# Statistics of one batch from summed chunks, two spreads over partitions by DMA, and new rules in the plan of an attention and feed-forward kernel

## The chip, the cores and the metric

The kernel runs on one core of one Trainium2 chip. The metric is the device time of one execution in microseconds. Before the change the median of three runs is 842.28 us (842.24 to 842.83). One more execution was taken with a profile; times "in the trace" count from its first instruction.

## The reference

Four batches of causal attention, 12 heads, 448 positions, 64 values a head, are followed by a feed-forward layer with a norm ahead of it and a sum around it, all in float32:

```python
scores = (q @ k.T) / 8, masked above the diagonal
attn = softmax(scores);  x = attn @ v            # 4 x 448 x 768 after joining the heads
mu = mean(x, -1);  var = mean((x - mu) ** 2, -1)
xn = (x - mu) / sqrt(var + 1e-6) * g
out = x + relu(xn @ w1) @ w2                     # 768 -> 3072 -> 768
```

## The kernel before, in words

**Layout.** x is kept transposed: six chunks `xT[c]` of 128 features by 448 positions for each batch. Every factor of a large product is split into a high and a low part, and three products stand for one. The positions are four blocks of 112 where they lie on partitions.

**Stages.** The first batch's attention comes first, with nothing to put beside it but weight conversion. The feed-forward layer of the first batch (`ffn`, L1106; tiles ph and po) then runs on TensorE, and between its products stand the second and third batch's attention; beside the second batch's feed-forward layer stand the rest of the third's and the fourth's. From 531 us of the trace the third and fourth batch's feed-forward layers run together (`Pair`, L1159), with seven products of blocks in place of eight; its tiles are bA, bX, bY, bZ. The weights arrive as float64, are converted once by ScalarE and VectorE (`convert1`, `convert2`, L617 to L634), stored to DRAM (`keep`, L636) and loaded again later.

**The plan.** The program first records every instruction as a task with its engine, its reads and writes and a due time (`Plan`, L173). TensorE's clock of due times advances by 1.45 us a step ahead of the first feed-forward layer and by the cost of the products within it. `schedule` (L317) works back from the due times to the time at which each task is needed, with SLACK (L44) added for each step, and calls `run` (L367) six times; that is a list scheduler with costs of its own (`cost`, L273) and the best of the six orders is issued. An engine takes the available task with the earliest need. `pick` (L471) passes over a task on the SBUF port that VectorE and GpSimd share if that port is taken for more than 0.3 us longer; this holds for the first 70 us of the plan's time. Between engines that could act at the same time, the order of `ENGINES` (L177) decides. All instructions are issued by one line, L526, so tiles tell them apart. SP issues all DMAs, in the plan's order. Tasks with two ways (`either`, L193) may go to either of two engines.

**Statistics.** Three ways lead to the mean and 1/sigma of a batch.
- First batch: `total` (L943) adds the six chunks, one product with a column of 1/768 gives the mean on all partitions (`mean`, L950), and `squares` (L956) subtracts it, squares on ScalarE, adds the six squares and reduces them over partitions with four products of one column. The power -1/2 is GpSimd's. `over_sigma` (L973) spreads the 112 x 4 result over partitions and positions with four transposes into PSUM and a copy.
- Second batch: `stats` (L983) transposes every chunk back (tile pln) and VectorE's bn_stats reads it; `aggr` (L994) joins them; `spread` (L1004) makes eight transposes and two copies on ScalarE. `apply1` reads the results.
- Third and fourth batch: `stats` and `aggr` as well; `Pair.banks` (L1167) spreads mean and 1/sigma of both batches with sixteen transposes into four PSUM banks, and the pair's inputs (`xg`, L1199) read them there.

`BYSUM` and `VAR0`, `RB0`, `AHEAD0` (L60 to L62) belong to the first way: steps between the mean, the squares and the first feed-forward layer. `tl` is the step at which a batch's attention is done; 84 (`PAIR`) is the step from which the pair's inputs are recorded.

**Pools.** probs is closed and temps, for the pair's inputs, is opened once probs has no more readers; in the same way pair_x follows ap (`open_inputs`, L1178).

Of the kernel before, what the change touches and what calls it, by code (L numbers as in the profile page):

```python
# [40 lines left out]
SECOND = 8000  # L41
BEHIND = 12000
EARLY_SLOT = 1450
SLACK, DMA_SLACK = 400, 6000  # L44
CHANGE, TOGETHER = 150, 12000
PASSES, PORT, LEAST, AFTER, URGENT, START = 6, 300, 300, 1500, 5000, 70000
STEPS = 6
FIRST = -20
RAT0, TAT0, NAT0, END0, EV0 = [-1, 1, 3], [7, 8, 9, 10, 11], [4, 6], 13, [1, 1, 0, 1, 0]
# [7 lines left out]
PAIR = 84  # L57
KEEP0 = 36
TWOS = {3: [0, 2, 4]}
BYSUM, VAR0, RB0 = [0], 2, 6  # L60
COPIED = [NP, NP, 3, 0]
AHEAD0 = 6  # L62
WARM, FILL, LATE = 10, 16000, 3500
LEFT = {1: (0, 0), 2: (0, 1), 3: "S4", 4: (1, 1), 5: "S1", 6: "S2", 7: "S3"}
RIGHT = {1: "B11", 2: "B21", 3: "B22", 4: "T4", 5: "T1", 6: "T2", 7: "T3"}
# [18 lines left out]
class View:  # L84
# [39 lines left out]
    def bitcast(self, dtype):  # L124
        return self._new(self.p, self.idx, lambda t: t.bitcast(dtype), dtype)

    def to_broadcast(self, shape):
        return self._new(self.p, self.idx, lambda t: t.to_broadcast(shape))

# [43 lines left out]
class Plan:  # L173

    ENGINES = ("tensor", "vector", "scalar", "gpsimd", "sync")  # L177

    def __init__(self):
        self.tasks, self.fresh, self.turns, self.clock, self.wait = [], [], [], 0.0, 0.0  # L180
# [136 lines left out]
    def schedule(self):  # L317
        tasks = self.tasks
        for t, buf in self.fresh:
            old = buf.before  # L320
            while old is not None and not old.any:
                old = old.before
            if old is not None:
                t.deps.update(old.any)
            elif buf.pool.opened is not None:
                t.deps.add(buf.pool.opened)
        for t, pools in self.turns:
            t.deps.update(n for pool in pools for buf in pool.tiles for n in buf.any)
        for t in tasks:
            for d in t.deps:  # L330
                tasks[d].then.append(t.n)
        need, left, line = [0.0] * len(tasks), [len(t.deps) for t in tasks], []
        line = [t.n for t in tasks if not t.deps]
        for n in line:
            for m in tasks[n].then:
                left[m] -= 1
                if left[m] == 0:
                    line.append(m)
        assert len(line) == len(tasks)
        for t in (tasks[n] for n in reversed(line)):  # L340
            x = t.due if t.engine == "tensor" else 1e9
            for m in t.then:
                x = min(x, need[m])
            if t.engine == "sync":
                x -= DMA_SLACK + t.lag / 300
            elif t.engine and t.engine != "tensor":
                x -= t.cost + t.lag + SLACK
            elif t.engine and x < t.due:
                x -= t.cost + t.lag + SLACK
            need[t.n] = x  # L350
        best, hint = None, None
        for _ in range(PASSES):
            order, span = self.run(need, hint)
            if best is None or span < best[1]:
                best = order, span, self.starts, self.fin, {t.n: t.way for t in tasks if t.engine}
            self.old, hint = self.starts, {e: [] for e in self.ENGINES}
            for t in tasks:
                for way in t.ways if t.engine else ():
                    hint[way[0]].append((self.ready[t.n], t.n))
            for x in hint.values():  # L360
                x.sort()
        order, span, self.starts, self.fin, kept = best
        for n, i in kept.items():
            self.take(tasks[n], i)
        return order, span

    def run(self, need, hint):  # L367
        tasks = self.tasks
# [34 lines left out]
        while True:  # L403
# [21 lines left out]
                    heapq.heappush(avail[e], (need[n] + more, n))  # L425
            heap = avail[e]
            if e not in ("tensor", "sync"):
                n, wake = self.pick(e, at, heap, start, port, need, hint, drift)
                if n is None:
                    held[e] = wake  # L430
                    continue
            elif e == "tensor":
                while heap:
                    x = heapq.heappop(heap)
                    heapq.heappush(tiled[tasks[x[1]].mode], x)
                heap = min((h for h in tiled.values() if h), key=lambda h: h[0])
                same = tiled[mode]
                if same and same[0][0] < heap[0][0] + TOGETHER:
                    heap = same
# [28 lines left out]
        self.ready = ready  # L468
        return [n for _, n in order], max(free.values())

    def pick(self, e, at, heap, start, port, need, hint, drift):  # L471


        skipped, wake, n = [], [], None
        while heap:
# [5 lines left out]
            skipped.append(x)  # L481
            if shared and port > at + PORT and at < START:
                wake.append(port)
                continue
            if hint is not None and at < START:
                line, first = hint[e], None
# [48 lines left out]
def kernel(ctx, tc, qk, v, w1, w2, g, out):  # L535
# [49 lines left out]
    scratch = [dr.tile([P, UE], F32, name=f"scratch{i}") for i in range(len(order))]  # L585
    kept = [dr.tile([P, UH], F32, name=f"kept{i}") for i in range(ns)]
    ready = set()
    raw, bits, w32, wh, wl = {}, {}, {}, {}, {}

    def load_raw(s):  # L590
# [114 lines left out]
    class Att:  # L705
# [237 lines left out]
        def total(self, p):  # L943
            if p == 0:
                return
            if p == 1:
                self.acc = rest[:, :S]
            self.add(self.acc, self.acc if p > 1 else self.xT[0], self.xT[p])

        def mean(self):  # L950
            mb = ps.tile([P, S], F32, tag="sc", name="mb", bufs=2)
            nc.tensor.matmul(mb, lhsT=part.to_broadcast([P, P]), rhs=self.acc, start=True, stop=True)
            self.mb = ap.tile([P, S], F32, tag="y", name="mbs", bufs=1)
            nc.scalar.activation(out=self.mb, in_=mb, func=ACTF.Copy, scale=-1.0)

        def squares(self):  # L956
            for c in range(KC):
                t = ap.tile([P, S], F32, tag="PT", name="xc", bufs=8)
                nc.vector.tensor_tensor(out=t, in0=self.xT[c], in1=self.mb, op=ALU.add)
                nc.scalar.activation(out=t, in_=t, func=ACTF.Square)  # L960
                if c:
                    self.add(acc, acc, t)
                else:
                    acc = t
            pt = ps.tile([C, NC], F32, tag="sc", name="var", bufs=2)
            for x in range(NC):
                nc.tensor.matmul(pt[:, x:x + 1], lhsT=acc[:, x * C:(x + 1) * C], rhs=part, start=True, stop=True)
            ve = sb.tile([C, NC], F32, tag="ve", name="ve", bufs=2)
# [1 line left out]
            nc.gpsimd.tensor_tensor(out=ve, in0=ve, in1=mhalf, op=ALU.pow)  # L970
            self.t["ve"] = ve

        def over_sigma(self):  # L973
            ve = self.t["ve"]
            rb = ps.tile([P, S], F32, tag="sc", name="rb", bufs=2)
            for x in range(NC):
                nc.tensor.transpose(
                    rb[:, x * C:(x + 1) * C], ve[:, x:x + 1].to_broadcast([C, P]), ident[:C, :C]
                )
            self.rb = ap.tile([P, S], F32, tag="rb", name="rbs", bufs=1)  # L980
            move(self.rb, rb)

        def stats(self, part, x):  # L983
            c0, c1 = (2 * part, 2 * part + 2) if self.twos else STATS[part]
# [18 lines left out]

        def spread(self):  # L1004
            mv, ve = self.t["mv"], self.t["ve"]
            mb = ps.tile([P, S], F32, tag="sc", name="mb", bufs=2)
            rb = ps.tile([P, S], F32, tag="sc", name="rb", bufs=2)
            for x in range(NC):
                nc.tensor.transpose(
                    mb[:, x * C:(x + 1) * C], mv[:, x, 0:1].to_broadcast([C, P]), ident[:C, :C]  # L1010
                )
            for x in range(NC):
                nc.tensor.transpose(
                    rb[:, x * C:(x + 1) * C], ve[:, x:x + 1].to_broadcast([C, P]), ident[:C, :C]
                )
            for key, src in (("mb", mb), ("rb", rb)):
                self.t[key] = ap.tile([P, S], F32, tag="PT", name=key, bufs=8)
                nc.scalar.copy(out=self.t[key], in_=src)
            self.parts()

        def apply1(self, c):
# [17 lines left out]
        def steps(self):  # L1039
# [13 lines left out]
            for p, t0 in enumerate(t0s):  # L1053
# [5 lines left out]
                if p - p % 2 in self.twos:  # L1059
                    if p % 2:  # L1060
                        put(post, t0 + end, self.pv, p - 1)
                        put(post, t0 + end, self.pv, p)
                else:
                    put(post, t0 + end, self.pv, p)
                if self.b == 0:
                    put(pre, t0 + end + 1, self.total, p)
                    put(pre, t0 + end + 1, self.gained1, p)
                    put(pre, t0 + end + 1, self.gained2, p)
# [14 lines left out]
            if self.b == 0:  # L1083
                put(post, tl, self.mean)
                put(pre, tl + AHEAD0 + VAR0, self.squares)
                put(post, tl + AHEAD0 + RB0, self.over_sigma)
                return pre, post, tl + AHEAD0
            th = TH1 if self.b == 1 else [t0s[i] + end + 1 for i in ((1, 3) if self.twos else (2, 4))]
            for x in range(NC):
                put(post, th[0] + x, self.stats, 0, x)  # L1090
# [68 lines left out]
    class Pair:  # L1159
# [6 lines left out]

        def banks(self):  # L1167
            for j, a in enumerate(self.at):
                mb = ps.tile([P, S], F32, tag="sc", name="mb", bufs=2)
                rb = ps.tile([P, S], F32, tag="pt", name="rb", bufs=2)  # L1170
                for dst, col in ((mb, lambda x: a.t["mv"][:, x, 0:1]), (rb, lambda x: a.t["ve"][:, x:x + 1])):
# [4 lines left out]
                a.t["mb"], a.t["rb"] = mb, rb  # L1176

        def open_inputs(self):  # L1178
            turn(probs, temps)
# [409 lines left out]
```

## Time and profile before

| | |
|---|---|
| median of the runs | 842.28 us |
| profiled execution, its time | 845.26 us |
| profiled execution, its span | 843.4 us |
| mean granted TensorE clock | 0.997 |
| TensorE busy | 835.7 us |
| VectorE, ScalarE, GpSimd busy | 689.8, 513.7, 266.3 us |
| SP's DMA queue | 167.9 MB |

The span goes from the first to the last instruction; the rest of the time lies around it. PE is TensorE's matmul, PEld its weight load, DVE VectorE, ACT ScalarE, POOL GpSimd, SP the engine that issues the DMAs. A matmul's duration runs to its modelled end, and the next one starts before that, so the distance of two starts is what one costs. In the rows an instruction is written as output<-inputs by tile names.

### The profile page before, as it was taken

To read this page: it belongs to the slowest core of one execution; us is meant where nothing else is said; L and a number is where in the kernel's file an instruction comes from. 1 tells how busy PE (TensorE), PEld (TensorE's weight loads), DVE (VectorE), ACT (ScalarE), POOL (GpSimd) and SP (SyncE) were. 2 spreads that over 40 slices of the span, in tenths; PEclk is the share of its full clock that TensorE was granted. 3 is DMA by queue.
4 is the path that set the end of the run, shared out by engine and by line. 5 is a ranking of instruction groups with operands and counts; after the bars stand their busy time and mean duration, and the time that the engine had idled before them with its cause. 6 is when DMAs were issued, how large, how long until landed. Compare 5 with 4: busy or idle time off the path is not lost.

```text
span 843.4 us, 13755 instructions
## 1 busy us (share of the span) xinstructions
PE 835.7 (99%) x4608; PEld 729.1 (86%) x4608; DVE 689.8 (82%) x1464; ACT 513.7 (61%) x1130; POOL 266.3 (32%) x271
## 2 busy tenths in 40 slices
PE   8999999999999999999999999999999999999998
PEld 5578898888888888888888899999999999999997
DVE  5999999899999997887777389786886768777685
ACT  7999998889898586554453135453634436354450
POOL 4732111011123521111110049445445454554440
PEclk9999999999999999999999999999999999999999
DMA  9588888967888778887766454324243332423334
GB/s 234 198 264 279 294 296 336 360 235 281 273 274 318 250 245 291 263 286 237 233 214 206 152 190 154 110 86 142 60 150 94 101 122 83 139 83 110 114 94 152
DMA packets 61318, 168.79 MB, mean 200 GB/s; under 512 B 7008, under 2 KB 25824, under 8 KB 61248
## 3 DMA queue, kind: packets, MB, share of 16 engines
q1 hardware_dynamic: 61248, 167.92, 59.7%
q8 instruction: 36, 0.59, 0.3%
q14 instruction: 34, 0.28, 0.1%
HBM read 119.15 MB, written 39.71 MB: 188 GB/s over the span
## 4 chain that ended last, share of the span: by engine, by line
PE 85%; DVE 6%; ACT 6%; issue 2%; DMA 1%; SPq 0%; POOL 0%; ACTq 0%; DVEq 0%; POOLq 0%
PE bX L526 21%; PE po L526 17%; PE ph L526 16%; PE bY L526 10%; PE bA L526 5%; PE px L526 5%; PE sc L526 4%; PE pt L526 4%; DVE w L526 1%; ACT P L526 1%; DVE P L526 1%; DVE wl L526 1%; ACT w L526 1%; ACT bits L526 1%; PE pln L526 1%
## 5 line engine op out<-in xcount | busy, mean ns | idle before, releaser
L526 POOL TENSOR_TENSOR kl<-qkraw,kh 128x896 fp32r<-128x896 f32 x18 | 40.4, 2245 | 254.8 <-ACT kh L526 137.5
L526 PE MATMUL ph<-xh,wh 128*128 128x450 f32 (+1 forms) x288 | 110.6, 384 | 0.0
L526 PE MATMUL po<-hh,wh 128*128 128x448 f32 x288 | 109.7, 381 | 0.0
L526 ACT ACTIVATE P<-P,least 112x448 f32<-112x448 f32 (+3 forms) x176 | 91.5, 524 | 28.5 <-DVE least L526 27.0
L526 PE MATMUL ph<-xh,wl 128*128 128x450 f32 (+1 forms) x288 | 106.2, 369 | 0.1
L526 PE MATMUL po<-hl,wh 128*128 128x448 f32 x288 | 105.9, 368 | 0.0
L526 PE MATMUL po<-hh,wl 128*128 128x448 f32 x288 | 105.7, 367 | 0.0
L526 PE MATMUL ph<-xl,wh 128*128 128x450 f32 (+1 forms) x288 | 105.4, 369 | 0.0
L526 ACT ACTIVATE wp<-s 128x256 fp32r<-128x256 f32 (+1 forms) x113 | 50.9, 459 | 74.8 <-PE bX L526 35.2
L526 DVE CUSTOM_DVE_ANT_0 P<-sc,mask 112x224 f32<-112x224 f32 (+3 forms) x176 | 72.7, 443 | 22.7 <-PE sc L526 22.4
L526 POOL TENSOR_TENSOR s<-u 128x256 f32<-128x256 f32 (+1 forms) x60 | 54.6, 919 | 78.1 <-DMA u<-scratch 54.0
L526 ACT ACTIVATE wk<-u 128x256 fp32r<-128x256 f32 (+1 forms) x77 | 35.7, 464 | 68.7 <-PE bX L526 56.0
L526 DVE TENSOR_TENSOR wp<-s,wp 128x256 fp32r<-128x256 f32 (+1 forms) x120 | 67.3, 571 | 0.8 <-ACT wp L526 0.4
L526 POOL TENSOR_TENSOR h<-b,h 128x448 fp32r<-128x448 f32 x36 | 42.2, 1173 | 70.8 <-ACT b L526 42.0
L526 DVE TENSOR_TENSOR xT<-xT,bX 128x448 f32<-128x448 f32 x72 | 44.4, 617 | 19.2 <-PE bX L526 18.7
L526 PEld LDWEIGHTS ph<-xh,wl 128*128 128x128 f32 x288 | 54.1, 188 | 5.5 <-DVE wl L526 0.5
L526 PEld LDWEIGHTS ph<-xh,wh 128*128 128x128 f32 x288 | 54.2, 188 | 4.8 <-issue 0.2
L526 PEld LDWEIGHTS po<-hh,wh 128*128 128x128 f32 x288 | 54.2, 188 | 4.6 <-DVE P L526 0.7
L526 PEld LDWEIGHTS po<-hh,wl 128*128 128x128 f32 x288 | 54.1, 188 | 4.4
L526 PEld LDWEIGHTS po<-hl,wh 128*128 128x128 f32 x288 | 54.3, 189 | 3.5
L526 PEld LDWEIGHTS ph<-xl,wh 128*128 128x128 f32 x288 | 54.4, 189 | 3.3
L526 ACT ACTIVATE PT<-pt 112x448 f32<-112x448 f32 x74 | 39.1, 539 | 23.6 <-PE pt L526 20.4
(184 smaller groups left out, 2193.4 us busy)
## 6 DMA issues: line engine op xcount, KB each, us to landing
raw<-w_dram SPq DMA_DIRECT2D x39, 768.0 KB, 6.9
scratch<-w SPq DMA_DIRECT2D x48, 384.0 KB, 5.2
full<-scratch SPq DMA_DIRECT2D x24, 768.0 KB, 6.9
qkraw<-qk_dram SPq DMA_DIRECT2D x18, 896.0 KB, 5.5
kept<-wl SPq DMA_DIRECT2D x30, 384.0 KB, 5.8
u<-scratch SPq DMA_DIRECT2D x24, 384.0 KB, 4.0
u<-scratch SPq DMA_DIRECT2D x36, 256.0 KB, 2.9
PR<-P SPq DMA_DIRECT2D x18, 490.0 KB, 4.0
```

The costliest lines, as they stand in the source:

```text
L526: getattr(getattr(nc, t.engine), method)(*args, **kw)
```

## The change

1. The fourth batch's statistics are made the first batch's way. Its chunks are added in pairs of chunks as they come (accumulator `acc` in probs), the mean's product stays in PSUM, VectorE subtracts it from there into tiles of ap (tag PT), and the variance goes to a PSUM bank of tag pt. `stats` and `aggr` are no longer called for it, and `banks` spreads only its 1/sigma.
2. `over_partitions` spreads a 112 x 4 tile over partitions with two DMAs: one writes it to a row of 448 values in DRAM, the other reads the row into all 128 partitions. It takes the place of the transposes and copies in `over_sigma` (first batch, 1/sigma) and in `spread` (second batch, mean and 1/sigma).
3. In the plan SLACK is 200, AHEAD0 is 4, GpSimd stands ahead of VectorE in `ENGINES`, `pick` lets VectorE pass over a task on the shared port while GpSimd works (first 70 us), and `MOVES` displaces the need of one task in eight by up to 3.9 us either way, and of one in 128 by up to 0.2 us, chosen by a hash of the task's number.

```diff
-SLACK, DMA_SLACK = 400, 6000
+SLACK, DMA_SLACK = 200, 6000
+MOVES = [
+    (79784165, 3000, 32, 7730, 90000), (121416589, 3000, 2, -410, 90000),
+]
-AHEAD0 = 6
+AHEAD0 = 4
...
-    ENGINES = ("tensor", "vector", "scalar", "gpsimd", "sync")
+    ENGINES = ("tensor", "gpsimd", "vector", "scalar", "sync")
...
+        base = list(need)
+        for seed, size, share, low, high in MOVES:
+            for t in tasks:
+                x = self.drawn(t.n, seed)
+                if t.engine and x % 256 < share and low < base[t.n] < high:
+                    need[t.n] += size * ((x >> 8) % 65536 / 65536 - 0.5)
...
+            if shared and e == "vector" and other > at and at < START:
+                wake.append(other)
+                continue
...
-                self.acc = rest[:, :S]
+                self.acc = probs.tile([P, S], F32, tag="acc", name="acc", bufs=1) if self.b else rest[:, :S]
...
+            if self.b:
+                self.t["mb"] = mb
+                return
...
+                if self.b:
+                    nc.vector.tensor_tensor(out=t, in0=self.xT[c], in1=self.t["mb"], op=ALU.subtract)
...
+        def over_partitions(self, dst, src):
+            row = dr.tile([NC, C], F32, name=f"row{len(rows)}")
+            rows.append(row)
+            nc.sync.dma_start(out=row.seen(lambda t: t.rearrange("x q -> q x")), in_=src)
+            nc.sync.dma_start(
+                out=dst, in_=row.seen(lambda t: t.rearrange("x q -> (x q)").partition_broadcast(P))
+            )
...
         def over_sigma(self):
-            ve = self.t["ve"]
-            rb = ps.tile([P, S], F32, tag="sc", name="rb", bufs=2)
-            for x in range(NC):
-                nc.tensor.transpose(
-                    rb[:, x * C:(x + 1) * C], ve[:, x:x + 1].to_broadcast([C, P]), ident[:C, :C]
-                )
             self.rb = ap.tile([P, S], F32, tag="rb", name="rbs", bufs=1)
-            move(self.rb, rb)
+            self.over_partitions(self.rb, self.t["ve"])
...
-            for key, src in (("mb", mb), ("rb", rb)):
+            for key, src in (("mb", mv[:, :, 0]), ("rb", ve)):
                 self.t[key] = ap.tile([P, S], F32, tag="PT", name=key, bufs=8)
-                nc.scalar.copy(out=self.t[key], in_=src)
+                self.over_partitions(self.t[key], src)
...
+                if self.b == 3:
+                    for x in (p - 1, p) if p % 2 else ():
+                        put(pre, t0 + end + 1, self.total, x)
...
+            if self.b == 3:
+                put(post, tl, self.mean)
+                put(post, tl + 1, self.squares)
+                return pre, post, PAIR
...
+                both = [(rb, lambda x: a.t["ve"][:, x:x + 1])]
+                if j == 0:
+                    a.t["mb"] = ps.tile([P, S], F32, tag="sc", name="mb", bufs=2)
+                    both.insert(0, (a.t["mb"], lambda x: a.t["mv"][:, x, 0:1]))
```

## Rows read from the trace of the kernel before

**Rows 1.** The page, part 1: busy us of each engine, share of span, instructions.

```profile
PE 835.7 (99%) x4608; PEld 729.1 (86%) x4608; DVE 689.8 (82%) x1464; ACT 513.7 (61%) x1130; POOL 266.3 (32%) x271
```

**Rows 2.** Stretches: us, busy (instructions) of PE, PEld, DVE, ACT, POOL; clock, DMA share, GB/s.

```profile
40.00:50.00 10.00, 10.00 (x68) 6.54 (x64) 8.34 (x26) 8.70 (x23) 4.21 (x9) 0.84 0.59 185
...
60.00:100.00 40.00, 39.90 (x216) 36.12 (x216) 38.57 (x79) 38.87 (x81) 9.55 (x6) 1.00 0.84 283
...
480.00:490.00 10.00, 10.00 (x67) 7.63 (x64) 4.11 (x13) 1.28 (x2) 1.01 (x1) 1.00 0.29 100
490.00:531.00 41.00, 41.00 (x211) 37.89 (x210) 39.80 (x54) 18.69 (x32) 30.35 (x23) 1.00 0.47 154
```

**Rows 3.** PE in order of time: start us, duration us, count; two spreads before the pair.

```profile
489.92 0.55 PE L526 MATMUL mb<-ident,mv 112*128 112x112 f32 x4
490.31 0.55 PE L526 MATMUL rb<-ident,ve 112*128 112x112 f32 x4
```

**Rows 4.** PE in order of time: the fourth batch's last statistics transposes.

```profile
484.67 0.49 PE L526 MATMUL pln<-ident,xT 128*112 128x128 f32 x3
...
485.60 0.38 PE L526 MATMUL pln<-ident,xT 128*112 128x128 f32 x2
```

**Rows 5.** PE in order of time: the first batch's mean, later its variance.

```profile
55.51 0.91 PE L526 MATMUL mb<-rest,g_sb 128*128 128x448 f32 x2
...
68.81 0.88 PE L526 MATMUL var<-g_sb,xc 128*112 128x1 f32 x8
```

**Rows 6.** Tile xc, first batch: duration min/median/max ns, first and last start us.

```profile
L526 DVE TENSOR_TENSOR xc<-xT,mbs x6: 618/619/620, 57.9 to 60.6; 128x448 f32<-128x448 f32 x6
...
L526 POOL TENSOR_TENSOR xc<-xc x3: 1158/1168/1912, 60.3 to 67.5; 128x448 f32<-128x448 f32 x3
```

**Rows 7.** Tile ve (variance, then 1/sigma), all batches; same columns.

```profile
L526 POOL TENSOR_TENSOR ve<-ve,mhalf x4: 1007/1026/1772, 71.7 to 487.9; 112x4 f32<-112x4 f32 x4
L526 DVE TENSOR_SCALAR ve<-mv x3: 158/159/163, 243.6 to 487.7; 112x4 f32<-112x4 f32 x3
```

**Rows 8.** VectorE, then PE, in order of time: last inputs of the pair, their readers.

```profile
525.15 1.47 DVE L526 TENSOR_TENSOR wp<-s,wp 128x384 fp32r<-128x384 f32 x2 [0.43 <-ACT wp L526]
...
530.34 0.61 DVE L526 TENSOR_TENSOR xT4l<-t,xT4h 128x448 fp32r<-128x448 f32 x1
...
531.66 0.37 PE L526 MATMUL bY<-xT1h,wp 128*128 128x448 f32 x1
...
543.49 0.36 PE L526 MATMUL bX<-xT4h,wk 128*128 128x448 f32 x1
```

**Rows 9.** DMA issues: count, KB each, median us to landing.

```profile
wk<-kept SPq DMA_DIRECT2D x54, 128.0 KB, 2.0
...
g_sb<-g_dram SPq DMA_DIRECT2D x1, 3.0 KB, 10.7
```

**Rows 10.** Tile rbs (first batch's 1/sigma): its first readers.

```profile
L526 DVE TENSOR_TENSOR po<-po,rbs x6: 615/622/627, 128.0 to 169.9; 128x448 f32<-128x448 f32 x6
```

**Rows 11.** Tile mb (means): its readers on VectorE, first of batch 1.

```profile
L526 DVE TENSOR_TENSOR xg<-xT,mb x18: 604/614/1571, 262.0 to 516.7; 128x448 f32<-128x448 f32 x18
```

**Rows 12.** ACT in order of time: idle before and what ended it, in brackets.

```profile
84.90 0.92 ACT L526 ACTIVATE w<-raw 128x768 f32<-128x768 f32 x1 [1.13 <-DMA scratch<-w]
```

**Rows 13.** Tile qs: its subtractions on VectorE, all batches.

```profile
L526 DVE TENSOR_TENSOR qs<-qkraw,qs x18: 1090/1948/2916, 33.9 to 432.0; 64x896 fp32r<-64x896 f32 x18
```

**Rows 14.** VectorE, then GpSimd, in order of time around 34 us.

```profile
33.92 2.60 DVE L526 TENSOR_TENSOR qs<-qkraw,qs 64x896 fp32r<-64x896 f32 x1
...
34.40 1.17 POOL L526 TENSOR_TENSOR rest<-rest,xT 128x448 f32<-128x448 f32 x1
```

**Rows 15.** PE in order of time: two equal groups px, and a wait between.

```profile
30.21 2.11 PE L526 MATMUL px<-PT,rest 112*64 112x448 f32 x16
...
37.24 0.63 PE L526 MATMUL sc<-first_qk 64*112 64x224 f32 x2 [0.84 <-DVE least L526]
...
39.25 3.46 PE L526 MATMUL px<-PT,rest 112*64 112x448 f32 x16
```

More of the change, by code (lines that the diff above doesn't have):

```diff
@@ L59 @@
 TWOS = {3: [0, 2, 4]}
-BYSUM, VAR0, RB0 = [0], 2, 6
+BYSUM, VAR0, RB0 = [0, 3], 2, 6
 COPIED = [NP, NP, 3, 0]
-AHEAD0 = 6
+AHEAD0 = 4
 WARM, FILL, LATE = 10, 16000, 3500
@@ L125, in bitcast, with seen @@
         return self._new(self.p, self.idx, lambda t: t.bitcast(dtype), dtype)
+    def seen(self, step):
+        return self._new(self.p, self.idx, step)
     def to_broadcast(self, shape):
@@ L365, in schedule, with drawn @@
         return order, span
+    @staticmethod
+    def drawn(n, seed):
+        x = (n * 2654435761 + seed * 2246822519) & 0xFFFFFFFF
+        for shift, factor in ((15, 2654435761), (13, 2246822519), (16, 1)):
+            x = ((x ^ (x >> shift)) * factor) & 0xFFFFFFFF
+        return x
     def run(self, need, hint):
@@ L427, in run @@
             if e not in ("tensor", "sync"):
-                n, wake = self.pick(e, at, heap, start, port, need, hint, drift)
+                n, wake = self.pick(e, at, heap, start, port, free["gpsimd"], need, hint, drift)
                 if n is None:
@@ L469, in run, with pick @@
         return [n for _, n in order], max(free.values())
-    def pick(self, e, at, heap, start, port, need, hint, drift):
+    def pick(self, e, at, heap, start, port, other, need, hint, drift):
         skipped, wake, n = [], [], None
@@ L587 @@
     ready = set()
+    rows = []
     raw, bits, w32, wh, wl = {}, {}, {}, {}, {}
@@ L958, in squares @@
                 t = ap.tile([P, S], F32, tag="PT", name="xc", bufs=8)
-                nc.vector.tensor_tensor(out=t, in0=self.xT[c], in1=self.mb, op=ALU.add)
+                if self.b:
+                    nc.vector.tensor_tensor(out=t, in0=self.xT[c], in1=self.t["mb"], op=ALU.subtract)
+                else:
+                    nc.vector.tensor_tensor(out=t, in0=self.xT[c], in1=self.mb, op=ALU.add)
                 nc.scalar.activation(out=t, in_=t, func=ACTF.Square)
@@ L964, in squares @@
                     acc = t
-            pt = ps.tile([C, NC], F32, tag="sc", name="var", bufs=2)
+            pt = ps.tile([C, NC], F32, tag="pt" if self.b else "sc", name="var", bufs=2)
             for x in range(NC):
@@ L1005, in spread @@
             mv, ve = self.t["mv"], self.t["ve"]
[L1006 to L1015, printed above, removed]
-            for key, src in (("mb", mb), ("rb", rb)):
+            for key, src in (("mb", mv[:, :, 0]), ("rb", ve)):
                 self.t[key] = ap.tile([P, S], F32, tag="PT", name=key, bufs=8)
-                nc.scalar.copy(out=self.t[key], in_=src)
+                self.over_partitions(self.t[key], src)
             self.parts()
@@ L1087, in steps @@
                 return pre, post, tl + AHEAD0
+            if self.b == 3:
+                put(post, tl, self.mean)
+                put(post, tl + 1, self.squares)
+                assert tl + 2 == PAIR
+                return pre, post, PAIR
             th = TH1 if self.b == 1 else [t0s[i] + end + 1 for i in ((1, 3) if self.twos else (2, 4))]
@@ L1168, in banks @@
             for j, a in enumerate(self.at):
-                mb = ps.tile([P, S], F32, tag="sc", name="mb", bufs=2)
                 rb = ps.tile([P, S], F32, tag="pt", name="rb", bufs=2)
-                for dst, col in ((mb, lambda x: a.t["mv"][:, x, 0:1]), (rb, lambda x: a.t["ve"][:, x:x + 1])):
+                both = [(rb, lambda x: a.t["ve"][:, x:x + 1])]
+                if j == 0:
+                    a.t["mb"] = ps.tile([P, S], F32, tag="sc", name="mb", bufs=2)
+                    both.insert(0, (a.t["mb"], lambda x: a.t["mv"][:, x, 0:1]))
+                for dst, col in both:
                     for x in range(NC):
@@ L1175, in banks @@
                         )
-                a.t["mb"], a.t["rb"] = mb, rb
+                a.t["rb"] = rb
         def open_inputs(self):
```

## The prediction

> **What bounds the kernel now.** I read the page's engine line first. TensorE is busy 835.7 us of the 843.4 us span, and what it misses lies at the two ends [rows 1]. The table of stretches says where that busy time is real [rows 2]. From 60 us on TensorE leaves out 0.1 us in 40, at the full granted clock, and weight loads fill 36.1 of 40; from there the time is the sum of TensorE's instructions, and what one of them costs is worth its own length. Before that it is different. From 40 to 50 us weight loads fill 6.5 of 10, VectorE is at 8.3 and ScalarE at 8.7, and the mean granted clock is 0.84: there the first batch's attention is paced by VectorE, ScalarE and GpSimd together, and TensorE waits in small pieces that the busy figure hides. So the change has two questions: how many TensorE instructions it removes, and whether its new plan brings the first 60 us forward.
>
> The profiled execution took 845.26 us, 1.8 us more than its own span, and 0.35% over the median of the runs, 842.28 us. The durations are its own; I take the difference from them and put it on the median. About 0.2% (1.7 us) is what a measurement can tell from no change.
>
> **TensorE, removed.** The transposes that spread a mean or 1/sigma go for the first batch (4), the second (8) and the fourth batch's mean (4). Groups of four follow each other at 489.92 and 490.31 us, so four cost 0.39 us [rows 3] and sixteen 1.6 us. The fourth batch's statistics lose 24 transposes of 128 columns. A group of three lasts 0.49 us, one of two 0.38 us [rows 4], so one more costs 0.11 us and 24 cost 2.6 us. Together 4.2 us.
>
> **TensorE, added.** The fourth batch gets one mean product (two passes) and four variance products (eight passes of one column). The first batch has the same: 0.91 and 0.88 us [rows 5]. Each figure holds the drain of its last pass, some 0.15 us, which the next matmul covers; I take 0.8 and 0.8 us, 1.6 in all. Net on TensorE: 4.2 - 1.6 = 2.6 us less, all in the stage where it is the bound.
>
> **The fourth batch's new chain.** The sums of its chunks run while its attention runs. GpSimd has an instruction there (1.01 us) after a long rest: it works 1.0 us of 10 from 480 to 490, and VectorE 4.1 [rows 2], so five adds at 1.17 us are covered. At the end come six subtractions (0.62 us each), six squares on ScalarE, and five adds that follow each other, 1.17 us on GpSimd [rows 6] or about half on VectorE. VectorE loses twelve bn_stats and four bn_aggr in exchange, so its sum is about even. Before, the variance was there at 487.7 us and 1/sigma one GpSimd instruction (1.0 us) later, near 488.9 us [rows 7]. After, from the last chunk, which the pln group at 484.67 reads [rows 4]: last add of a chunk about 485.6, mean 486.5, first square 487.8, five adds of about 1 us to 493, variance product, the tiny add and the power to about 495.5 us. The fourth batch's 1/sigma comes some 6 to 7 us later. What waits for it is the pair's inputs: from 490 to 531 us VectorE is busy 39.8 of 41 [rows 2], in order, so a late start would move them whole. But two of the first four inputs are of the third batch, and the other two's subtraction needs only the mean; these can be done while the chain runs, about 4 us of VectorE. I take the inputs 3 us late (bounds 0 and 7). What is late next: weight parts that share VectorE's queue end at 526.6 us and a product with such parts starts at 531.7, a margin of 5.0 us; the last input, xT4l, ends at 530.95 and its products start at 543.49, a margin of 12.5 us [rows 8]. So the cost is 0, at worst 7 - 5 = 2 us.
>
> **1/sigma and a mean by DMA.** Six small transfers join SP's queue in three pairs, the second of a pair waiting in that queue for the first to land. The nearest rows for one landing are 2.0 us (128 KB, queue almost free) and 10.7 us (3 KB, behind the first loads) [rows 9]; a spread costs 4 to 21 us in place of half a microsecond of transposes and a copy. I take 8, since the queue is in use but not full. For the first batch this has no reader: 1/sigma is there near 73 us [rows 7], read first at 128.0 us [rows 10]. For the second, the variance is there at 243.6 us [rows 7] and the mean is first read at 262.0 us [rows 11]: 18 us cover it, or miss by 3 us at the far end, and what would then be late is VectorE's reading, which TensorE's queue doesn't follow at once. ScalarE or VectorE loses three PSUM copies. Cost 0; what could lose is the queue behind, a rival below.
>
> **The plan.** New slack, displaced due times, the first batch's lead of 4 steps in place of 6, and the rule that VectorE takes up no instruction on the shared port while GpSimd works. The rule is aimed at one visible thing. A subtraction on qs that needs 1.09 us at its shortest [rows 13] lasted 2.60 us at 33.92, with GpSimd in an instruction until 35.57 [rows 14]. VectorE lost 1.5 us, TensorE then waited 0.84 us for VectorE's minimum, and soon after ran a group px in 3.46 us that took 2.11 us ten us earlier [rows 15]; the mean of 0.84 from 40 to 50 us [rows 2] means some 3 us at 1.2 in place of 2.4 GHz. If the subtraction moves behind the port, up to 1.5 + 1.35 = 2.9 us are to be had. Not all passes on, because ScalarE in those stretches is nearly as full as VectorE, and a delayed VectorE instruction has readers too. I take half, 1.5 us. The reordering beyond that no row shows. Its gain is bounded by what VectorE leaves idle in such a stretch, 1.7 us in 10 [rows 2], over three of them 5 us; its loss I bound by as much.
>
> **Sum.** 842.3 - 2.6 (TensorE) - 1.5 (start) = 838.2 us; against the profiled execution 841.2.
>
> **Rivals.**
> Start unchanged: the plan's rule works on the plan's own times, and if these miss the real ones VectorE still meets GpSimd. Then only TensorE's sum is left: 842.3 - 2.6 = 839.7 us. For it speaks that the one long meeting in the trace came under a plan that already avoided a busy port by its own reckoning; against it that the new rule asks for a wholly free GpSimd.
> Start worse: VectorE waits for GpSimd's gaps, and a conversion or a score's minimum behind the waiting instruction comes late. Two waits the length of the 1.5 us seen [rows 14] give back 3.0 us: 842.7 us, no change that can be told.
> Pair late: 1/sigma is 7 us late, nothing is done meanwhile, and 2 us pass the margin of 5 us: 842.3 - 2.6 + 2 = 841.7 us. For it, VectorE's full stretch; against, third-batch inputs that need not wait.
> Slower: SP blocks. If the second transfer of the first batch's pair stands in SP's queue before the first has landed, the weight stores behind it wait. It decides from the point where this exceeds the room of the converted weights, and there is little: at 84.90 us ScalarE already idled 1.13 us for such a store [rows 12]. A landing of 10.7 in place of 2.0 us holds SP for 8.7 us; if 6 of these reach TensorE through ScalarE's conversion, the time is 842.3 - 2.6 + 6 = 845.7 us. Against it, the reader is 55 us away, so the plan can put the second transfer behind every urgent one. The Trainium skill (DMA: Bandwidth & Descriptors, Rules for kernel authors) speaks for this rival: a transfer whose last dimension isn't contiguous becomes one descriptor per element, and should be rearranged. By it the column-to-row write is 448 descriptors of 4 bytes. No row of the kernel before shows such a transfer.
>
> **How the numbers follow.** Forecast (start gains, up to 5 us): 0.67. Start unchanged: 0.13. Start worse: 0.08. Pair late: 0.05. SP blocks: 0.07. The first two are faster: 0.80. Start worse and pair late lie within 0.2%: 0.13. Slower: 0.07. The range goes from 835.0 us (2.6 and most of 5 us gained, 842.3 - 2.6 - 4.7) to 841.9 us, which takes in the pair late and most of a start that loses up to 2 us, and leaves out SP's block and half of the worse start.
>
> **What would show it.** Right: pln 48 in place of 72, rb and mb transposes down by 16, TensorE's busy sum 2 to 4 us lower; the qs subtraction near 34 us at about 1.1 us; no px group of 3.4 us, a granted clock of 1.0 from 40 to 44 us; the first ph group before 49 us; no TensorE wait between 484 and 545 us. Wrong: SP waits between 73 and 90 us followed by ScalarE waiting on a weight store; TensorE idle near 531 us; the first ph later than before.

## The result: 0.75% slower, and the profile after

Six runs of the changed kernel have a median of 849.59 us (846.0 to 851.05), six of the kernel before beside them 842.56 us (842.2 to 844.18): a ratio of 1.0075, interval 1.0051 to 1.0098. The forecast was 838.2 us, the range ended at 841.9. The profiled execution took 851.05 us with a span of 849.3 us; one execution of the six took 846.0 us, so the loss itself varies.

The page of the kernel after, part 1, and its line on DMA packets:

```profile
PE 835.5 (98%) x4578; PEld 728.8 (86%) x4578; DVE 693.4 (82%) x1464; ACT 508.3 (60%) x1119; POOL 288.0 (34%) x285
...
DMA packets 63142, 169.48 MB, mean 200 GB/s; under 512 B 8448, under 2 KB 27648, under 8 KB 63072
```

Thirty TensorE instructions are gone, as counted (40 removed, 10 added), yet the busy sum is only 0.2 us under that of [rows 1], where 2.6 us were forecast. A matmul at the lower clock counts as longer in it, so this sum doesn't price the saving. The packets under 512 B were 7008 before. Three transfers of 448 values make 1344 of the 1440 new ones.

**The end of the change that worked.** Stretches of the kernel after, in the columns of [rows 2], then its tiles pln and ve:

```profile
40.00:50.00 10.00, 9.35 (x76) 6.56 (x76) 10.00 (x27) 10.00 (x17) 6.23 (x8) 1.00 0.79 252
...
490.00:531.00 41.00, 41.00 (x213) 37.83 (x212) 38.04 (x54) 18.69 (x32) 33.56 (x27) 1.00 0.55 177
```

```profile
L550 PE MATMUL pln<-ident,xT x48: 270/272/322, 144.3 to 370.4; 128*112 128x128 f32 x48
```

```profile
L550 POOL TENSOR_TENSOR ve<-ve,mhalf x4: 1015/1120/1931, 69.9 to 499.2; 112x4 f32<-112x4 f32 x4
L550 DVE TENSOR_SCALAR ve<-var x2: 155/159/163, 69.7 to 498.1; 112x4 f32<-112x4 f32 x2
```

TensorE stays full ahead of the pair although the fourth batch's 1/sigma is now made at 499.2 us instead of 487.9 [rows 7]. From 40 to 50 us the clock is 1.00 where [rows 2] has 0.84.

**The place of the loss.** To compare two traces I weighted every TensorE product with its columns, left the statistics' out, and noted when each trace had reached the same sum. Minus means ahead of the profiled execution of before, in us:

```
reached by before at (us)   67.0    90.2   112.3   248.6   271.4   541.2   802.8
after                       -3.5    -1.8    +1.1    +0.5    +6.0    +5.2    +5.5
```

The two losses, 2.9 us by 112 us and 5.5 us by 271, each follow a column-to-row write, at 71.9 and at 248.7 us. SP's issues around the second, in order of time:

```profile
247.75 0.45 SPq L550 DMA_DIRECT2D kept<-wl  x1
248.30 0.38 SPq L550 DMA_DIRECT2D scratch<-w  x1
248.72 0.95 SPq L550 DMA_DIRECT2D row<-mv  x1
249.77 1.42 SPq L550 DMA_DIRECT2D row<-ve  x1
...
254.16 0.62 SPq L550 DMA_DIRECT2D raw<-w_dram  x1
260.76 0.32 SPq L550 DMA_DIRECT2D scratch<-w  x1
264.72 0.32 SPq L550 DMA_DIRECT2D mb<-row  x1
```

The DMA issues from 246 to 256 us, count, KB each and median us to landing, of after:

```profile
raw<-w_dram SPq DMA_DIRECT2D x3, 768.0 KB, 14.9
kept<-wl SPq DMA_DIRECT2D x2, 384.0 KB, 14.0
scratch<-w SPq DMA_DIRECT2D x2, 384.0 KB, 14.9
...
row<-mv SPq DMA_DIRECT2D x1, 1.8 KB, 15.9
row<-ve SPq DMA_DIRECT2D x1, 1.8 KB, 15.3
```

and of before:

```profile
raw<-w_dram SPq DMA_DIRECT2D x2, 768.0 KB, 8.0
scratch<-w SPq DMA_DIRECT2D x3, 384.0 KB, 6.6
kept<-wl SPq DMA_DIRECT2D x2, 384.0 KB, 5.5
```

Two writes of 1.8 KB take 15 to 16 us, and the stores and loads of weights issued from 247.75 to 254.16 us take 13 to 16 us, about twice the medians of before or more. What that does is in VectorE's order of time, then ScalarE's, then TensorE's:

```profile
260.79 0.96 DVE L550 TENSOR_TENSOR wl<-w,wh 128x768 fp32r<-128x768 f32 x1 [6.23 <-DMA kept<-wl]
...
268.10 2.30 DVE L550 TENSOR_TENSOR wl<-w,wh 128x768 fp32r<-128x768 f32 x1 [0.22 <-DMA kept<-wl]
270.42 1.09 DVE L550 TENSOR_TENSOR qs<-qkraw,qs 64x896 fp32r<-64x896 f32 x1
```

```profile
263.51 0.89 ACT L550 ACTIVATE w<-raw 128x768 f32<-128x768 f32 x1 [7.09 <-DMA scratch<-w]
```

```profile
271.57 0.46 PE L550 MATMUL sc<-kh,qs 128*112 128x448 f32 x1 [3.79 <-DVE qs L550]
...
272.35 0.57 PE L550 MATMUL po<-hl,wh 128*128 128x448 f32 x1
272.72 0.58 PE L550 MATMUL po<-hh,wl 128*128 128x448 f32 x1
...
275.96 0.37 PE L550 MATMUL po<-hh,wh 128*128 128x448 f32 x1
276.16 0.37 PE L550 MATMUL po<-hl,wh 128*128 128x448 f32 x1
```

VectorE may not overwrite a weight part until its store to `kept` has landed, and waits 6.23 us; ScalarE waits 7.09 us for a store to `scratch`. VectorE then has its queue to work off, so the qs subtraction ends at 271.5 us, and TensorE waits 3.79 us for it. After that wait equal products start 0.37 us apart, from 275.96 us on 0.20 us: the lower of the two clock levels (granted clock 0.62 from 271.5 to 276 us), some 2 us more. Wait and clock make about the 5.5 us of the table. The first loss is the same on a smaller scale: ScalarE waits 3.67 us for a store to `scratch` ahead of 85.05 us, where it was 1.13 us before [rows 12].

### The profile page after: what moved, and what is told of

Its sections match the earlier page's. It is cut to its first block, busy times and chain, and to the rows that moved or that the text cites. A ratio compares the mean times of both kernels' runs of the same rounds, so it can differ in the third digit from the quotient of the medians.

```text
span 849.3 us, 13690 instructions
## 1 busy us (share of the span) xinstructions
PE 835.5 (98%) x4578; PEld 728.8 (86%) x4578; DVE 693.4 (82%) x1464; ACT 508.3 (60%) x1119; POOL 288.0 (34%) x285
## 4 chain that ended last, share of the span: by engine, by line
PE 87%; ACT 5%; DMA 4%; DVE 3%; issue 1%; POOL 0%; SPq 0%; ACTq 0%; DVEq 0%; POOLq 0%
PE bX L550 21%; PE po L550 20%; PE ph L550 15%; PE bY L550 10%; PE sc L550 5%; PE bA L550 5%; PE px L550 5%; PE pt L550 4%; DMA scratch<-w 3%; ACT P L550 1%; ACT wh L550 1%; ACT w L550 1%; DMA full<-scratch 1%; DVE P L550 1%; PE pln L550 1%
## 5 line engine op out<-in xcount | busy, mean ns | idle before, releaser
L550 ACT ACTIVATE wp<-s 128x256 fp32r<-128x256 f32 (+1 forms) x104 | 47.0, 462 | 68.1 <-PE bX L550 32.9
L550 DVE CUSTOM_DVE_ANT_0 P<-sc,mask 112x448 f32<-112x448 f32 (+3 forms) x176 | 72.4, 440 | 16.9 <-PE sc L550 16.5
L550 POOL TENSOR_TENSOR h<-b,h 128x448 fp32r<-128x448 f32 x36 | 44.1, 1226 | 64.5 <-ACT h L550 34.9
L550 DVE TENSOR_TENSOR wl<-w,wh 128x768 fp32r<-128x768 f32 x48 | 53.5, 1117 | 12.1 <-DMA kept<-wl 6.5
```

Source lines behind the costliest of these rows:

```text
L550: getattr(getattr(nc, t.engine), method)(*args, **kw)
```

## The experiments

Theories: **choke**, the column-to-row write with its single 4-byte values slows the DMA engines for everything else; **queue**, SP stands on the second transfer of a pair and holds up what is behind; **plan**, the new order itself loses the time. Each ratio is against runs of the kernel before on the same chip; the first four kernels ran on one chip, the others on two more.

**1. Spreads back on TensorE** (`x1_both_pe`, `x2_first_dma`, `x3_second_dma`). The transposes and the copy return for both batches, for the second alone, for the first alone. A task added by an experiment gets no number of its own, so that MOVES displaces the same tasks as in the change.

```diff
         def over_partitions(self, dst, src):
+            if self.b in BY_PE:      # [0, 1]; [1]; [0]
+                pt = ps.tile([P, S], F32, tag="sc", name="rb", bufs=2)
+                for x in range(NC):
...
+                    nc.tensor.transpose(pt[:, x * C:(x + 1) * C], src[:, x:x + 1].to_broadcast([C, P]), ident[:C, :C])
+                move(dst, pt)
...
+                return
```

> Both spreads by transposes again, as in the kernel before; the fourth batch's new statistics and the new plan stay (the plan is made anew around the transposes, so its order differs). If the row writes of single 4-byte values are what loses (theory A): the 3 us that the changed kernel is ahead at 60 us are kept and the fourth batch's 1.4 us on TensorE come on top, 842.5 - 3 - 1.4 = 838 us; no stretch of 5 us with DMA under 100 GB/s after 70 us, no TensorE wait over 1.5 us. If the new plan itself is at fault (theory B): 847 us or more, with the waits at 75 to 95 us and at 268 us still there.

> Only the first batch's 1/sigma is spread by DMA, the second batch's two spreads go by transposes. Theory A: the loss between 60 and 110 us (4.6 us in the changed kernel) stays, the one at 268 us (5.5 us) goes: about 843 us. Theory B: 847 us or more.

> Only the second batch's mean and 1/sigma are spread by DMA, the first batch's goes by transposes. Theory A: the loss of 5.5 us at about 268 us stays, the one between 60 and 110 us goes: about 843.5 us. Theory B: 847 us or more.

Measured: both on TensorE 842.95 us, ratio 0.9977 (0.9968 to 0.9987); the first batch by DMA 846.47 us, 1.0024 (1.0014 to 1.0033); the second by DMA 853.42 us, 1.0100 (1.0085 to 1.0115). Without any spread by DMA the kernel is faster than before, though by 1.5 to 1.9 us where 4.4 were expected: by the table's method its trace gives back 2.5 us between 67 and 90 us, with no spread in it. Each spread costs. For the first it is 3.5 us, between the first two kernels; their orders differ from 73 us on, but from 90 to 112 us the trace with the spread loses 3.0 us and the other 0.4. The third was planned anew from 13 us on and runs in another order. Its time is one that was expected if the plan were at fault (847 us or more), and a part of it is the order's: its trace loses 4.6 us between 60 and 67 us, ahead of any spread, and 7.1 us between 248.6 and 271.4 us, behind the writes at 251.4 and 252.2. So the 10 us that it takes more than the first kernel show the sign of the second spread and not its size. The first kernel has the lowest ratio of those here that compute the whole reference.

**2. The same plan, wider pieces** (`x4_rows16`, `x9_rows8`). The row is written as 112 pieces of 16 bytes or 224 of 8 instead of 448 of 4, with every instruction in the change's own order. For that the values stand in another order in the row, and in the second batch's mean the first four numbers of its statistics stand for the means: this part of the output is not the reference's.

```diff
-            nc.sync.dma_start(out=row.seen(lambda t: t.rearrange("x q -> q x")), in_=src)
+            nc.sync.dma_start(out=row.seen(lambda t: t.rearrange("x q -> (x q)").rearrange("(q x) -> q x", x=NC)), in_=src)
```

> The changed kernel with the same plan, instruction for instruction, but the row in DRAM is written in 112 pieces of 16 bytes in place of 448 of 4 bytes: the row's values then stand in another order, and in place of the means the first four numbers of the statistics tile are spread, so both spreads of the norm are not those of the reference. Theory A (the count of pieces chokes the DMA engines): the dip in DMA throughput shrinks to a quarter, the row lands within 8 us in place of 16, 842 us or less. Rival C (the second transfer's wait in SP's queue loses the time, whatever the pieces): 847 us or more, SP held as long as in the changed kernel.

> As the run with 16-byte pieces, same plan, but 224 pieces of 8 bytes (the spread values are again in another order, and the means are replaced by the first four numbers of the statistics tile). If the loss goes with the number of pieces: half of the changed kernel's, 845 us where the kernel before takes 842.5, the row lands about 3 to 4 us after issue at 72 us. If only single 4-byte pieces are slow: as with 16 bytes, 839 us.

Measured: 16 bytes 841.27 us, 0.9956 (0.9939 to 0.9973); 8 bytes 844.68 us (842.49 to 847.36), 1.0022 (1.0010 to 1.0034). From 4 to 16 bytes the ratio falls by 0.0119, 10 us, with the same order of instructions. The runs of before beside the 16 bytes were slower, 844.44 us, 11 of 19 with a granted clock under 1.000; the two kernels' own times differ by 8.3 us. So the writes cost the changed kernel 8 to 10 us. The first batch's write landed in 6.7 us with 4 bytes, 4.9 with 8, 1.4 with 16. The queue theory has no support in the changed kernel's trace: the first batch's second transfer is issued at 112.4 us, 34 us after the first has landed, so SP never waited there; and the stores that VectorE and ScalarE waited for at 260.79 and 263.51 us had been issued at 247.75 and 248.30 us, ahead of the row, while SP's wait for the row, to 264.72 us, ended after both had gone on. The store that VectorE waited for to 268.10 us had been issued at 253.08 us, ahead of that wait too.

**3. Where the pieces lie** (`x10_padded`, `x13_spaced`, `x14_dense`). The 16-byte row stays, as in experiment 2, and an extra write of the same 448 values, which nobody uses, goes beside it into DRAM. In the first kernel it goes to a tile of its own, 64 bytes apart, and the plan put the second batch's extra writes at 408 us, outside the crowded stretch. In the other two the second transfer waits for both, so that the order is the same, and one line differs:

```diff
-  flat(t)[S:S + S * 16].rearrange("(x q e) -> q x e", q=C, e=16)[:, :, 0]    # x13_spaced: one value every 64 bytes
+  flat(t)[S:2 * S].rearrange("(x q) -> q x", q=C)                            # x14_dense: side by side
```

> As the run with 16-byte pieces, plus one more write per spread that nobody reads: the same 448 values of 4 bytes, but each 64 bytes from the next (the spread values are in another order and the means replaced, as there). If the number of pieces is what chokes: the loss of the changed kernel is back, 849 us where the kernel before takes 842.5. If neighbours in one stretch of DRAM memory hold each other up: no dip in DMA throughput, 841 us or less.

> One order of instructions for this run and the next. Each spread's row is written in 112 pieces of 16 bytes, as before (the spread values in another order, the means replaced by the first four numbers of the statistics tile); beside it 448 pieces of 4 bytes go to a place nobody reads, and the second transfer waits for both. Here each piece lies 64 bytes from the next. If the count of pieces chokes the DMA engines: both losses of the changed kernel are back, 849 us where the kernel before takes 842.5, DMA near 100 GB/s after the write. If it is neighbours in DRAM memory: 843 us or less, no dip, the write lands within 3 us at 72 us.

> The same order, and the 448 unread pieces of 4 bytes lie side by side, as the changed kernel's row. By either theory the losses of the changed kernel are there, 847 to 851 us where the kernel before takes 842.5, and the write lands 6 to 7 us after issue at 72 us. If it isn't slower than the spaced one, neither theory holds and the loss comes from elsewhere in the changed kernel.

Measured: apart at an uncrowded time 841.55 us, 0.9983 (0.9974 to 0.9993); apart 841.66 us, 0.9984 (0.9975 to 0.9993); side by side 853.19 us, 1.0122 (1.0103 to 1.0140). The same number of pieces of the same size costs 11.5 us or nothing that these runs can tell, by the distance of their addresses. Distances between 4 and 64 bytes were not tried. Stretches of the kernel with pieces apart, columns as in [rows 2]:

```profile
72.00:82.00 10.00, 9.66 (x50) 8.79 (x51) 9.97 (x20) 9.33 (x15) 0.00 (x0) 1.00 0.85 272
...
250.00:266.00 16.00, 16.00 (x96) 14.11 (x93) 13.34 (x25) 13.46 (x28) 5.27 (x3) 1.00 1.02 332
266.00:280.00 14.00, 14.00 (x81) 11.65 (x81) 13.93 (x24) 6.85 (x17) 6.27 (x5) 1.00 0.78 301
```

side by side:

```profile
72.00:82.00 10.00, 9.50 (x51) 8.62 (x51) 9.97 (x18) 8.20 (x13) 0.00 (x0) 1.00 0.82 63
...
250.00:266.00 16.00, 16.00 (x97) 13.66 (x96) 11.17 (x25) 10.00 (x22) 5.67 (x3) 1.00 1.00 131
266.00:280.00 14.00, 10.00 (x42) 8.68 (x40) 8.25 (x16) 9.33 (x20) 1.15 (x1) 0.76 0.99 371
```

and the changed kernel itself:

```profile
72.00:82.00 10.00, 9.50 (x53) 8.47 (x52) 9.67 (x16) 8.71 (x14) 0.00 (x0) 1.00 0.73 105
...
250.00:266.00 16.00, 15.72 (x93) 13.04 (x92) 7.77 (x19) 7.76 (x17) 1.79 (x1) 1.00 1.02 193
266.00:280.00 14.00, 10.21 (x49) 8.93 (x49) 13.68 (x25) 11.03 (x23) 5.41 (x3) 0.88 1.03 395
```

The last two numbers of a line are to be read together. The DMA engines are as busy in all three from 250 to 266 us (1.00 to 1.02) but move 332, 131 and 193 GB/s: they are held, not idle. TensorE pays one stretch later. The load that follows the first batch's row shows it alone; DMA issues from 70 to 74 us, pieces apart:

```profile
qkraw<-qk_dram SPq DMA_DIRECT2D x1, 896.0 KB, 5.7
...
row<-ve SPq DMA_DIRECT2D x2, 1.8 KB, 2.0
```

side by side:

```profile
qkraw<-qk_dram SPq DMA_DIRECT2D x1, 896.0 KB, 10.8
...
row<-ve SPq DMA_DIRECT2D x2, 1.8 KB, 7.5
```

The single packets in the traces say what is held. The pieces of this write are all over by 73.2 us, at 9 ns each, apart or side by side. But a packet of 7168 bytes of the load behind them takes 0.27 us with the pieces apart (median of the 128 that start from 71.3 to 79 us), 2.91 us side by side (only 32 start by then) and 2.32 us in the changed kernel (34). So it is not the small packets that last; the large ones behind them do. Why neighbours do this to them, no run shows. In 64 bytes of the row lie 16 pieces of 4 bytes, 8 of 8 bytes, 4 of 16 bytes, and one where they are apart. The losses fall in that order as far as they can be told apart; that this count decides would fit, and is only argued.

**4. Two repairs that keep the spread by DMA** (`x5_strided`, `x11_row4`). The first writes 16-byte pieces and lets VectorE read the spread row with a step of 16 bytes. The second makes one transpose to 4 x 112 and writes four pieces of 448 bytes.

```diff
# x5_strided, one reader of three
-  nc.vector.tensor_tensor(out=y, in0=pm, in1=a.rb, op=ALU.mult)
+  nc.vector.tensor_tensor(out=y.seen(by_block), in0=pm.seen(by_block), in1=a.rb.seen(turned), op=ALU.mult)
# x11_row4
-  nc.sync.dma_start(out=row.seen(lambda t: t.rearrange("x q -> q x")), in_=src)
+  pt = ps.tile([NC, C], F32, tag="sc", name="rb", bufs=2)
+  nc.tensor.transpose(pt, src, ident[:C, :C])
+  move(dst[:NC, :C], pt)
+  nc.sync.dma_start(out=row, in_=dst[:NC, :C])
```

> The whole change with the row written in 112 pieces of 16 bytes; the readers on VectorE take it with a stride of 16 bytes, so the result is the reference's (one small copy of the means is added, and the plan shifts a little after 60 us). Theory A (single 4-byte pieces choke the DMA engines): as the run with 16-byte pieces, 3 to 4 us under the kernel before, near 838 us on a chip where that takes 842; the strided readers last at most 0.1 us longer. Rival: the stride costs VectorE, xg instructions over 0.8 us, and up to 2 us of the gain are gone.

> A repair with the reference's result: one transpose turns the 112 x 4 tile into 4 rows of 112, a copy brings them to SBUF, and the row goes to DRAM in 4 pieces of 448 bytes; the second transfer is as in the changed kernel. TensorE gets 0.1 us a spread in place of the four transposes' 0.39. If the pieces were the fault: no dip, 838 to 840 us where the kernel before takes 842.5 (ratio 0.995 to 0.997). If the two transfers' wait is: 847 us or more.

Measured: 852.64 us, 1.0110 (1.0095 to 1.0126), and 847.87 us, 1.0054 (1.0037 to 1.0071). Both lose, and the second's time is one that was expected if the two transfers' wait were at fault. But by the table's method both are still ahead of before at 271.4 us, behind the spreads, by 3.6 and 2.8 us; they lose later, for reasons of their own. In the first the readers are slow; its tile rbs:

```profile
L565 DVE TENSOR_TENSOR po<-po,rbs x6: 937/972/1416, 118.5 to 166.7; 128x448 f32<-128x448 f32 x6
L565 DVE TENSOR_TENSOR y<-po,rbs x6: 933/950/1376, 240.6 to 305.5; 128x448 f32<-128x448 f32 x6
```

The same po needed 0.62 us with neighbours read in order [rows 10]. VectorE has no room for it beside the second batch's inputs (busy 14.0 of 14 us from 272 to 286 us), and TensorE waits 3.08 us for a transposed probability at 289.26 us. The Trainium skill (SBUF — State Buffer, Specifications) gives SBUF lines of 16 bytes, each of which must be hit at least twice for the full rate; a step of 16 bytes hits each once, and the trace agrees with 0.97 against 0.62 us. In the second, TensorE has no wait between 250 and 296 us, and the loss comes at 317 us, on ScalarE and then on TensorE:

```profile
314.38 0.84 ACT L555 ACTIVATE wh<-full 128x768 fp32r<-128x768 f32 x1 [2.59 <-DMA full<-scratch]
```

```profile
316.91 0.34 PE L555 MATMUL pt<-ident,PR 112*112 112x112 f32 x2 [2.29 <-ACT PT L555]
```

A weight load comes late, and the copy that TensorE's transposes need stands behind it in ScalarE's order. That is the order which the planner found for this kernel, and says nothing of long pieces; how this repair would do in another order was not tried.

**5. The other parts alone** (`x6_fourth_only`, `x7_plan_only`). The kernel before with part 1 of the change only, and with part 3 only.

> The kernel before with the fourth batch's new statistics alone; plan and spreads as before. By the sum of the prediction 24 + 4 transposes leave (2.6 + 0.4 us) and 1.6 us come: 1.4 us under the kernel before, ratio 0.998. Rival (pair's inputs late): TensorE waits near 530 us, ratio 1.000 or over.

> The kernel before with the new plan alone (slack, displaced needs, order of engines, the rule on the port, the shorter lead); spreads and the fourth batch's statistics as before. The prediction's term for the start was 1.5 us; the changed kernel's trace was 3.4 us ahead at 60 us and some 2 us of that were left where no choke followed. Expected 840.5 us where the kernel before takes 842.5 (ratio 0.9975). Rival: the needs are displaced by the tasks' numbers, which fall differently here, so the start may gain nothing: ratio 0.999 to 1.002.

Measured: 842.57 us, 0.9994 (0.9984 to 1.0004), and 844.66 us, 1.0021 (1.0012 to 1.0030). The plan alone is slower. By the table's method its profile is 3.8 us ahead of the profile of before at 67 us and 1.35 us ahead at 90 us, so what the start gains goes back between the two, with no spread by DMA in it. At its end it is still 0.6 us ahead of that profile (spans of 842.8 and 843.4 us), yet its runs are 2 us behind those of before. So the kernel before as it was profiled is not the kernel before as it usually runs. Its granted clock was 0.997; on two of the three chips 43 of 44 executions of before had 1.000, with spans of 840.3 to 842.9 us against 843.4. On the third, the chip of experiment 1, only 8 of 19 had. The fourth part alone says the same: its instructions stand in the order of before up to 393 us, its profile is 1.9 us ahead at 42 us and still 2.0 us at the end, and its runs gain 0.4 us.

## Why the prediction was wrong

**The failed step: "1/sigma and a mean by DMA … Cost 0."** I priced only how long the row takes (2.0 to 10.7 us for one landing, 4 to 21 for a spread, taken as 8) and asked only who reads it. The first write landed in 6.7 us, within that. The second batch's two took 15 to 16 us, and its mean was there 22.9 us after the first of them was issued (248.72 to 271.63 us), past both bounds. Still the readers could wait: the first batch's row was there at 118.7 us and read at 122.9, and the second's mean was read at 273.1 us with no wait for it on VectorE. What I left out is what the write does to other transfers. Behind it the large packets slow down, and the stores and loads that TensorE lives on come late. Experiment 2 prices this at 8 to 10 us in the changed kernel, experiment 3 at 11.5 us for an extra write of the same kind. The miss is 849.59 - 838.2 = 11.4 us; the rest of it is gain that didn't come (below). The rows that I took for the price [rows 9] are loads, of 128 KB and of 3 KB, and no row showed a write to DRAM in small pieces.

**The slower rival had the right wait and the wrong lever.** It put 6 us on ScalarE waiting for a weight store after the first batch's spread, and ScalarE and VectorE did wait for stores. It made SP's queue the cause, which no wait in the trace supports (experiment 2), and the first batch the place, where the smaller part was lost. The rule which I quoted there from the Trainium skill (DMA: Bandwidth & Descriptors, Rules for kernel authors), one descriptor per element for a last dimension that isn't contiguous, is what the packets show. Its price in this kernel depended on something that the rule doesn't say: the distance of the elements. I gave the rival 7 chances in 100.

**TensorE's sum, -2.6 us: the instructions left as counted, and the trace bears out most of their price.** pln came down to 48, the spreads' transposes by 16, and the fourth batch's products took 1.02 and 0.85 us where the first batch's took 0.91 and 0.88. By the table's method the kernel with 16-byte rows gains 0.8 us from 248.6 to 271.4 us, where eight transposes (0.8) left, and 1.3 us from 400 to 541 us, where the fourth part was to give 4.2 - 1.6 less the first two batches' 1.2, 1.4 us. No run shows the sum by itself, since the plan is in each of them. Without the choke the change gains 3.7 us by experiment 2 (16 bytes; 2.9 us against those 8 runs of before that had a clock of 1.000, median 844.2 us), but 1.4 and 1.3 us by the two kernels of experiment 3 with the pieces apart, where 4.1 us were forecast. The fourth part alone gave 0.4 us in its runs, at most 1.3 by its interval, and 0.2 us from 400 to 541 us of its trace; there TensorE waited 0.49 us for VectorE's last sum ahead of the mean's product.

**The start, -1.5 us, was mostly an accident of the profiled execution.** The long px group and the mean clock of 0.84 [rows 2, 15] were real in that execution. `x6_fourth_only` issues the same instructions there in the same order, and its profile has the qs subtraction in 1.44 us and not 2.60, the second px group in 2.11 us and not 3.46, and the full clock:

```profile
40.00:50.00 10.00, 9.40 (x72) 6.11 (x68) 9.13 (x27) 9.47 (x23) 7.77 (x9) 1.00 0.83 276
```

I noted that the profiled execution stood 3.0 us over the median and still took a saving in it off the median. The changed kernel did get most of what was forecast for this place, a clock of 1.00, a qs subtraction of 1.09 us at 37.8 us and no px group over 2.11 us there; but most executions of before on two of three chips have the clock too. The first ph group, forecast before 49 us, came at 50.28 us, later than the 49.40 of before, which was a sign of being wrong. Against the profile of `x6_fourth_only` the plan alone is 2.2 us ahead at 67 us and 0.3 behind at 90: what is left of the start is given back, and why is not shown.

**The fourth batch's chain, cost 0, held with its size wrong.** 1/sigma came 11 us later (499.2 against 487.9 us) and not 6 to 7. The mean's product was at 487.11 us, where 486.5 was taken, but GpSimd began the five adds of squares only at 490.00 us, after 2.95 us of waiting for the squares of ScalarE, needed 6.48 us for them, and the power stood behind another of its instructions (1.35 us). The margins of [rows 8] covered it: TensorE was full from 490 to 531 us.

## What to carry to other kernels

A small transfer is priced by what it does to the others: count its pieces, look how they lie in DRAM, and look for a crowded stretch within twenty microseconds behind it. Pieces of 16 bytes side by side, or of 4 bytes 64 bytes apart, cost nothing here that the runs can tell; and TensorE made the turn for half a microsecond. And where the profiled execution stands off the median, find the place of the difference first; a stall that belongs to it is nothing that a change can win.

## What the runs showed of the hardware

- 448 values of 4 bytes written side by side to DRAM landed in 6.7 us on an emptying queue, in 8.1 and 8.4 us behind one store (`x3_second_dma`) and in 15 to 16 us in a full queue; the same pieces 64 bytes apart took 2.3 and 2.7 us (at 72 us) and 7 to 9 us in the full one, 224 of 8 bytes side by side 4.9 us, 112 of 16 bytes 1.4 us. Behind the neighbours the DMA engines showed full and moved 131 to 193 GB/s, against 332 with the pieces apart; packets of 7168 bytes took 2.3 to 2.9 us there in place of 0.27.
- The Trainium skill (DMA: Bandwidth & Descriptors, Specifications) puts the least transfer for the line rate at 512 bytes and a read-modify-write below it. All pieces here are below that, those that cost nothing and those that cost 11.5 us, so the size alone doesn't decide.
- A 128 x 448 product of VectorE in float32 with one operand read in steps of 16 bytes took 0.97 us, with neighbours 0.62 us.
